# Attention, MoE and routed MoE in one kernel: batch 0's gate logits as VectorE sums over rows read back, and expert 0's w1 loaded whole

## The chip, the cores and the metric

The kernel runs on one core of a Trainium2 chip. The metric is the device time of one execution in microseconds. "Before" is the median of three runs; one further execution was recorded by the hardware profiler, and every row below is from it. Engines are named as in the profile: PE is TensorE's matmul stream, DVE is VectorE, ACT is ScalarE, POOL is GpSimd, and SP is SyncE, which here only issues DMAs.

## What is computed

Attention with a decay over 4 batches of 576 tokens and 8 heads gives x with 2304 rows of 512. Then comes a dense MLP, and then an MLP of 8 experts, 288 tokens each. The expert of a token comes from a greedy walk over all 2304 x 8 gate logits in falling order, so that an exact order of the logits matters.

```python
h = np.maximum(x @ w_in, 0.0)            # _moe_ref: 512 -> 2048
x = (h * h @ w_out).astype(np.float32)   # 2048 -> 512, "x2" below

logits = x @ w_gate                      # _moe2_ref: 512 -> 8
order = np.argsort(-logits.flatten())
for idx in order:                        # first come, first served, 288 tokens each
    tok, e = (int(idx) // E, int(idx) % E)
    if assigned[tok] >= 0 or counts[e] >= cap:
        continue
    assigned[tok] = e
    counts[e] += 1
for e in range(E):
    mask = assigned == e
    out[mask] = np.maximum(x[mask] @ w1[e], 0.0) @ w2[e]
```

## The kernel before

**Stages.** Attention runs by batch and head; its result goes to a DRAM buffer `xd` and is read back as `xa`. The dense MLP works in chunks of 256 tokens: two chunks of batch 0 first, then two of batch 1, two of batch 2 and one of batch 3 (`moe1_chunk`); the last two chunks (`moe1_last`) run together. The batch-0 chunks run while attention of the later heads is still at work, up to about 290 us. The float32 operands are split into a high and a low part (`hh`, `hl` of the hidden values, `xh`, `xl` of the inputs), and each product is three matmuls (L693 to L695 up, L717 to L719 down). Each hidden tile goes PE, then ACT (relu, L698), then a square (L699), then a rounding to `hh`, then a subtraction to `hl` (L710), which VectorE or GpSimd does; the down matmul L719 waits for `hl`.

**Where x2 and the logits come from.** When a chunk is done, its two tiles of 128 tokens are taken from PSUM and stored to `x2d` in DRAM, from which the experts gather their rows later. The logits are made in one of three ways:
- `x2_tail` (batches 0 and 3): 4 transposes on PE (L823), a copy, 8 small matmuls against w_gate (L831; one instruction each of 4 in the listing of the program, 8 in the trace), a copy into `L`.
- `x2_sums` (batches in `DL`, here 1 and 2): 8 instructions on VectorE for a tile (L798), each a multiply with one column of w_gate laid out over all partitions (`wgb`) and a sum over the 512 elements; each is followed by a read of the accumulator.
- in `moe1_last`: from the hidden values through `G2`, the product of w_out and w_gate. `gate_weights` makes `G2` on VectorE beforehand: 16 additions (L850) and 128 of the same sums (L853), which is what VectorE mostly does from about 300 us on. `G2` is finished by L858 and first used by a matmul at about 569 us.

**Who sets the order.** Each engine's order is fixed when the program is built. A list planner places every operation by priority (`s.base`, smaller first) and by modelled durations. `after=` and `hold` are only known to this planner; the hardware waits only for data and buffers. `hi` and `lo` operations have several candidate engines, of which the planner takes one.

**The experts.** The routing of expert m finds its number; SP then reads that number into a register (a value load, L1192) and issues loads of w1 and w2 from that expert's slice (L1204, four tiles each, 512 KB a tile). Before, w1 of the first expert is loaded in halves of 256 KB: the first halves of two tiles when its number is known, the first halves of the other two behind the last x2 store (`WX = 2`, `after=self.x2_done`), all second halves behind the gather. The gather (L1185) is an indirect DMA that GpSimd issues, three of 96 rows of `x2d`. Then PE transposes the rows (L1252) and multiplies (L1272).

Of the kernel before, what the change touches and what calls it, by code (L numbers as in the profile page):

```python
# [8 lines left out]
F = mybir.dt.float32  # L9
R = mybir.dt.float32r  # L10
BF = mybir.dt.bfloat16
# [8 lines left out]
B, H, S, D = 4, 8, 576, 64  # L20
NT, DM, DFF, E, FE = 2304, 512, 2048, 8, 1024
# [11 lines left out]
RS = [("z", z) for z in (31, 30, 29)]  # L33
WS = [("z", 28)]
TM = 1
WX = 2
P0 = None
HV = [0]
NSM = 4

DL = (1, 2)
ABASE = (0, 0.5, 0.6, 2)
HM = 50.0
LM = 40.0
# [278 lines left out]
def dve1(n):  # L323
    return 70 + 1.04 * n
# [46 lines left out]
class K:  # L371
# [355 lines left out]
    def moe1_chunk(self, b, c):  # L727
# [14 lines left out]
        for t in range(2):  # L742
            (self.x2_sums if b in DL else self.x2_tail)(b, c, t, acc[t])

# [45 lines left out]

    def x2_sums(self, b, c, t, acc):
        s = self.s
        xr = s.buf(self.xp, [128, DM], F, "x2g", 0, also=[("xo", 0), ("xo", 1)])
        xr.after = self.gp.bar
        xr, tt = self.x2_rows(b, c, t, acc, xr)
        for x in range(E):
            jk = s.buf(self.gp, [128, DM], BF, "gjs", 1)
            s.op({"dve": dve1(DM) + 285}, lambda e, x=x, jk=jk: e.tensor_tensor_reduce(  # L798
                out=jk.t, in0=xr.t, in1=self.wgb[:, x, :], scale=1.0, scalar=0.0, op0=OP.mult, op1=OP.add,
                accum_out=self.L[:, tt, x:x + 1]), r=[xr, self.wgb], w=[jk, (self.L, tt)])  # L800

    def x2_rows(self, b, c, t, acc, xr=None):
        s, mp = self.s, self.mp
        xr = xr or s.buf(mp, [128, 512], F, "x2r", 0, also=[("wraw", 0), ("wraw", 1)])
        s.op({"act": act(512, True), "dve": dve1(512)}, lambda e: self.rnd(e, xr.t, acc.t), r=[acc], w=[xr])
        tt = (b * 4 + c * 2 if b < B else 16) + t
        if b < B:
            tok = b * S + 64 + c * 256 + t * 128
            self.dma(lambda: self.x2d[tok:tok + 128, :], lambda: xr.t, 128 * 2048, r=[xr], w=[(self.x2d, tt)])
        else:  # L810
            for j in range(2):
                tok = (2 * t + j) * S
                self.dma(lambda tok=tok: self.x2d[tok:tok + 64, :], lambda j=j: xr[64 * j:64 * j + 64], 64 * 2048, r=[xr], w=[(self.x2d, (tt, j))])
        return xr, tt
# [361 lines left out]
    def expert(self, m, idx, widx):  # L1176
        s, nc, ep = self.s, self.nc, self.ep
# [5 lines left out]
        def gather_x():  # L1183
            for g in range(3):
                s.op({"pool": 1040.0}, lambda e, g=g: e.indirect_dma_start(  # L1185
                    out=xg[:, g, :], out_offset=None, in_=self.x2d.t, in_offset=IO(ap=idx[:, g:g + 1], axis=0)),
                    r=[idx, self.x2d], w=[(xg, g)], nbytes=96 * 2048)
# [39 lines left out]
        if m:  # L1227
            for i in range(4):
                wload(0, i)(0, 2)
            s.base = XB + m  # L1230
            gather_x()
            s.base = 30 + m
            for i in range(4):
                wload(1, i)(0, 2)
        else:
            loads = [wload(0, i) for i in range(4)]
            for i in range(4):
                loads[i](0, 1 if 0 in HV else 2, after=self.x2_done if WX <= i else None)
            s.base = X0
            gather_x()  # L1240
            s.base = 30 + m
            if 0 in HV:
                for i in range(4):
                    loads[i](1, 2, hold=True)
            for i in range(4):
                wload(1, i)(0, 2, hold=True)
        s.base = (XB + m if m else X0)
        xh, xl = [], []
        for k in range(4):
            pt = s.buf(self.ps, [128, 512], F, "xt", 0, also=XT + (XA if m == 0 else []))  # L1250
            for g in range(3):
                s.op({"pe": 107.0}, lambda e, k=k, g=g, pt=pt: e.transpose(pt[:, 96 * g:96 * g + 96], xg[:, g, k * 128:k * 128 + 128], self.ident[:96, :96]),  # L1252
                     r=[(xg, g), self.ident], w=[pt])
# [39 lines left out]
        for d in range(4):  # L1293
            acc = s.buf(self.ps, [128, 512], F, "y", 0, also=YA)
# [141 lines left out]
```

## Time and profile before

| | us |
|---|---|
| median of 3 runs | 995.26 |
| the three runs | 993.12, 995.26, 998.85 |
| the profiled execution | 997.44 |
| its span, first to last instruction | 995.7 |

| engine | busy, share of the span |
|---|---|
| PE | 929.3 us, 93% |
| DVE | 637.0 us, 64% |
| ACT | 392.1 us, 39% |
| POOL | 344.9 us, 35% |

The mean granted TensorE clock is 0.972 of full speed. A time in a row is measured from the start of the span. In a line of the timeline the first number is the start, the second the length (of a whole run of like instructions, where xN stands), and the bracket at the end is the idle time of that engine just before, with what ended it.

### The profile page before, as it was taken

What the parts mean: (1) busy time and instruction counts of PE and PEld (TensorE: products, weight loads), DVE (VectorE), ACT (ScalarE), POOL (GpSimd) and SP (SyncE); (2) the same over time, 40 slices, a digit from 0 to 9 for tenths busy, and PEclk for the clock granted to TensorE, in tenths of its full rate; (3) what the DMA queues carried; (4) which work ended last, traced back from release to release, by engine and by line L of the source; (5) the groups of instructions that cost most, each with busy time, mean ns of one, the idle gap of its engine ahead of it and who ended that gap; (6) DMA issues with size and microseconds to landing.
All of it is one profiled execution on the core that took longest, in us unless ns stands there. A gap on an engine that the chain in (4) does not pass through costs nothing. (4 is left out here: it accounts for less than half of the span.)

```text
span 995.7 us, 17474 instructions
## 1 busy us (share of the span) xinstructions
PE 929.3 (93%) x6135; PEld 749.8 (75%) x6135; DVE 637.0 (64%) x2037; ACT 392.1 (39%) x1068; POOL 344.9 (35%) x459
## 2 busy tenths in 40 slices
PE   6897899899999999999999999994999979999996
PEld 3554455677779898989989899774777867778995
DVE  6999888984438999992627322576767786422231
ACT  4665567655634444444343366200101021224320
POOL 2555555653333425341313100001113050557921
PEclk9999899999999999999999999996999998999998
DMA  6668677642230101010100000007735450334410
GB/s 215 206 222 266 197 238 248 194 136 85 75 129 24 44 1 43 1 44 1 43 15 9 22 1 2 11 33 214 241 134 201 176 175 22 111 110 151 133 48 24
DMA packets 48615, 105.66 MB, mean 106 GB/s; under 512 B 10280, under 2 KB 18632, under 8 KB 48400
## 3 DMA queue, kind: packets, MB, share of 16 engines
q1 hardware_dynamic: 45456, 95.11, 29.0%
q0 software_dynamic: 3072, 9.44, 3.2%
q8 instruction: 48, 0.79, 0.3%
q14 instruction: 39, 0.32, 0.1%
HBM read 90.20 MB, written 14.33 MB: 105 GB/s over the span
## 5 line engine op out<-in xcount | busy, mean ns | idle before, releaser
L693 PE MATMUL u<-xh,z 128*128 128x256 f32 x512 | 147.6, 288 | 2.4 <-ACT r L698 1.9
L694 PE MATMUL u<-xh,z 128*128 128x256 f32 x512 | 144.8, 283 | 0.0
L695 PE MATMUL u<-xl,z 128*128 128x256 f32 x512 | 144.7, 283 | 0.0
L698 ACT ACTIVATE r<-u 128x256 f32<-128x256 f32 x144 | 54.6, 380 | 162.7 <-PE u L695 138.0
L710 POOL TENSOR_TENSOR hl<-r,hh 128x256 fp32r<-128x256 f32 x79 | 74.7, 947 | 117.4 <-ACT hh L385 100.7
L853 DVE CUSTOM_DVE_ANT_0 gjk<-wof,wgb 128x512 bf16<-128x512 f32 x128 | 108.1, 845 | 11.0 <-DMA wgb<-wgT 8.0
L693 PEld LDWEIGHTS u<-xh,z 128*128 128x128 f32 x512 | 97.2, 190 | 15.3 <-issue 3.1
L694 PEld LDWEIGHTS u<-xh,z 128*128 128x128 f32 x512 | 97.4, 190 | 8.0
L695 PEld LDWEIGHTS u<-xl,z 128*128 128x128 f32 x512 | 97.3, 190 | 0.0
L1301 PE MATMUL acc<-ehh,z 128*128 128x288 f32 x320 | 91.8, 420 | 0.0
L719 PE MATMUL acc<-z,hl 128*128 128x512 f32 x224 | 88.6, 396 | 2.9 <-POOL hl L710 2.1
L717 PE MATMUL acc<-z,hh 128*128 128x512 f32 x224 | 90.1, 402 | 0.0
L718 PE MATMUL acc<-z,hh 128*128 128x512 f32 x224 | 89.2, 398 | 0.0
L1272 PE MATMUL u<-exh,z 128*128 128x288 f32 x304 | 87.0, 422 | 0.1
L1224 POOL TENSOR_TENSOR z<-wr,z 128x512 fp32r<-128x512 f32 x48 | 61.3, 1312 | 48.1 <-ACT z L385 48.0
L525 ACT ACTIVATE p<-p,st 128x448 f32<-128x448 f32 (+4 forms) x109 | 59.9, 550 | 37.7 <-DVE st L518 37.4
L513 POOL TENSOR_TENSOR row<-maskb,row 128x128 f32<-128x128 bf16 (+1 forms) x90 | 45.8, 516 | 69.0 <-DVE st L518 48.4
L1301 PEld LDWEIGHTS acc<-ehh,z 128*128 128x128 f32 x320 | 57.5, 194 | 16.3 <-issue 2.0
L1272 PEld LDWEIGHTS u<-exh,z 128*128 128x128 f32 x304 | 55.8, 195 | 14.8 <-DVE exh L389 0.3
L1185 POOL DMA_INDIRECT xg<-x2d,ph_idx x24 | 25.6, 1065 | 99.4 <-DVE ph_P L1127 51.9
L699 ACT ACTIVATE r<-r 128x256 f32<-128x256 f32 x139 | 58.0, 418 | 4.2
L1324 POOL DMA_INDIRECT out_dram<-yo,ph_idx x24 | 24.3, 1011 | 100.8 <-DVE ph_q L1034 32.7
(354 smaller groups left out, 2199.2 us busy)
## 6 DMA issues: line engine op xcount, KB each, us to landing
z<-in_w_dram SPq DMA_DIRECT2D x36, 512.0 KB
wr<-in_w_dram SPq DMA_DIRECT2D x24, 512.0 KB
z<-in_w_in_dram SPq DMA_DIRECT2D x16, 512.0 KB
z<-in_w_out_dram SPq DMA_DIRECT2D x14, 512.0 KB
row<-cumd SPq DMA_DIRECT2D x24, 288.0 KB
xd<-xo SPq DMA_DIRECT2D x16, 288.0 KB
wraw<-rd SPq DMA_DIRECT2D x32, 128.0 KB
xa<-xd SPq DMA_DIRECT2D x8, 512.0 KB
```

The lines of the kernel that those rows point to most:

```text
L525: s.op({"act": act(w, extra=2)}, lambda e, x=x, si=si, i=i, n=n, w=w, p=p[x], st=st[x]: e.activation(p[:n, :w], p[:n, :w], AF.Exp, bias=st ...
L693: e.matmul(u[:, :256], wh[:, k % 2, fs], xh[k][1](), start=(k == 0), stop=False)
L694: e.matmul(u[:, :256], wl[:, k % 2, fs], xh[k][1](), start=False, stop=False)
L695: e.matmul(u[:, :256], wh[:, k % 2, fs], xl[k][1](), start=False, stop=(k == 3))
L710: s.op(lo_alts(256), lambda e: e.tensor_sub(hl(), r.t, hh().bitcast(F)), r=[r, kh], w=[kl])
L717: g = [lambda e: e.matmul(acc.t, hh()[:, ts], wh[:, f % 2], start=(f == 0), stop=False), lambda e: e.matmul(acc.t, hh()[:, ts], wl[:, f % ...
L718: lambda e: e.matmul(acc.t, hh()[:, ts], wl[:, f % 2], start=False, stop=False),
L719: lambda e: e.matmul(acc.t, hl()[:, ts], wh[:, f % 2], start=False, stop=(f == 15))]
L853: s.op({"dve": dve1(DM) + 85}, lambda e, f=f, x=x, wo=wo, jk=jk: e.tensor_tensor_reduce(out=jk.t, in0=wo.t, in1=wb[:, x, :], scale=1.0, sc ...
L1224: s.op(lo_alts(512, LOE(m, which, i, 0, c)), lambda e, cs=cs: e.tensor_sub(lo[:, cs], raw[:, cs], hi[:, cs].bitcast(F)), r=[(raw, key), (h ...
L1272: s.op({"pe": 1.69 * CAP}, lambda e, k=k: e.matmul(u[:, :CAP], whi[0][k][:, fs], xh[k].t, start=(k == 0), stop=(k == 3)), r=[(whi[0][k], c ...
L1301: e.matmul(acc[:, :CAP], wh[:, ds], hh.t, start=(f == 0), stop=(f == 7))
```

## The change

Three constants and two functions change. `DL` becomes (0, 1, 2), so batch 0's two chunks (four tiles) take `x2_sums` in place of `x2_tail`. For batch 0 the tile is stored to `x2d` as before, from the same kind of buffer (`wraw`), and then read back from `x2d` into a buffer "x2k" in the space of the attention outputs `xo`; the eight sums of each tile work on that copy and write their products to a buffer of their own ("gjk0"). The read-back and the sums stand at priority 10. Second, `WX` and the split into halves are gone for expert 0: its four w1 tiles are issued whole, one after the other.

```diff
-WX = 2
-DL = (1, 2)
+DL = (0, 1, 2)
     def x2_sums(self, b, c, t, acc):
-        xr = s.buf(self.xp, [128, DM], F, "x2g", 0, also=[("xo", 0), ("xo", 1)])
+        xr = s.buf(self.xp, [128, DM], F, "x2g" if b else "x2k", 0, also=[("xo", 0), ("xo", 1)])
         xr.after = self.gp.bar
-        xr, tt = self.x2_rows(b, c, t, acc, xr)
+        base = s.base
+        if b:
+            xr, tt = self.x2_rows(b, c, t, acc, xr)
+        else:
+
+            _, tt = self.x2_rows(b, c, t, acc)
+            s.base = 10
+            tok = b * S + 64 + c * 256 + t * 128
+            self.dma(lambda: xr.t, lambda: self.x2d[tok:tok + 128, :], 128 * 2048, r=[(self.x2d, tt)], w=[xr])
         for x in range(E):
-            jk = s.buf(self.gp, [128, DM], BF, "gjs", 1)
+            jk = s.buf(self.gp, [128, DM], BF, "gjs" if b else "gjk0", 1)
...
+        s.base = base
...
             for i in range(4):
-                loads[i](0, 1 if 0 in HV else 2, after=self.x2_done if WX <= i else None)
+                loads[i](0, 2)
             s.base = X0
             gather_x()
             s.base = 30 + m
-            if 0 in HV:
-                for i in range(4):
-                    loads[i](1, 2, hold=True)
```

Line numbers of the changed kernel differ: L798 becomes L805, L850 and L853 become L858 and L861, L1192 becomes L1200, L1204 becomes L1212, and lines from 389 to 719 go down by one.

On PE, in the stretch where batch 0's first chunk ends, the order before is this (u and pt are PSUM tiles; L823 is the transpose of an x2 tile, L557 a transpose of attention, L693 to L695 an up product):

```order
939 L557 MATMUL pt_3660<-ident,p_3601 128x128 x3
940 L557 MATMUL ov_3661<-ident,p_3614 128x128 x3
941 L823 MATMUL u_3671<-ident,wraw_3658 128x128 x4
942 L693 MATMUL u_3567<-xh_3552,z_310 128x256
943 L694 MATMUL u_3567<-xh_3552,z_340 128x256
```

and after the change:

```order
939 L556 MATMUL pt_3660<-ident,p_3601 128x128 x3
940 L556 MATMUL ov_3661<-ident,p_3614 128x128 x3
941 L692 MATMUL u_3567<-xh_3552,z_310 128x256
942 L693 MATMUL u_3567<-xh_3552,z_340 128x256
943 L694 MATMUL u_3567<-xl_3572,z_310 128x256
```

The four transposes are gone, and so are those of the three other tiles of batch 0 and the four groups of logit matmuls (L831); the rest of the PE's matmuls to the end of the dense MLP are the same.

On VectorE, where the first sums stand, the order after the change is this ("ISA ... 128x512" is a sum, the "ISA ... 128x1" behind it the read of its accumulator; L805 is a logit of batch 0 from the row tile xo, L861 a sum of `gate_weights`):

```order
725 L805 ISA gjk_3932,L<-xo_3826,wgb_3845 128x512
726 L805 ISA L 128x1
727 L861 ISA gjk_3939,gf_3940<-wof_3796,wgb_3845 128x512
728 L861 ISA gf_3940 128x1
729 L805 ISA gjk_3951,L<-xo_3826,wgb_3845 128x512
730 L805 ISA L 128x1
731 L861 ISA gjk_3964,gf_3940<-wof_3796,wgb_3845 128x512
732 L861 ISA gf_3940 128x1
```

Before, only the sums of `gate_weights` stood in a row here. Further on, where the chunk is that ran at 470 us, the order before is this (L710 makes the `hl` that a down product waits for, L680 an `xl`):

```order
1074 L710 TENSOR_TENSOR hl_5822<-r_5808,hh_5817 128x256
1075 L710 TENSOR_TENSOR hl_5845<-r_5831,hh_5840 128x256
1076 L699 TENSOR_TENSOR r_5862<-r_5862 128x256
1077 L680 TENSOR_TENSOR xl_5872<-xa_4275,xh_5869 128x256
1078 L710 TENSOR_TENSOR hl_5882<-r_5862,hh_5877 128x256
```

and the same hidden tile after:

```order
1109 L861 ISA gjk_5852,gf_3940<-wof_5708,wgb_3845 128x512
1110 L861 ISA gf_3940 128x1
1111 L698 TENSOR_TENSOR r_5859<-r_5859 128x256
1112 L861 ISA gjk_5869,gf_3940<-wof_5708,wgb_3845 128x512
1113 L861 ISA gf_3940 128x1
1114 L709 TENSOR_TENSOR hl_5883<-r_5859,hh_5876 128x256
```

The sums of `gate_weights`, which before ended at the L858 above these rows, now reach beyond them. Counted over the whole listing, before has 152 sums, 14 additions and 6 other operations from the first sum to L858; after has 183 sums, 14 additions and 9 other operations from the first sum to the `hl` of row 1114. The 9 others after are 3 subtractions for `hl`, 4 for `xl` and 2 squares; the 6 before are 4 `hl`, one `xl` and one square. Up to the hidden tile of these rows VectorE makes 13 `hl` before and 4 after: nine go to GpSimd (79 before, 88 after over the whole kernel).

On SP, near `wgb` (the copy of w_gate over all partitions that every sum reads) the order before is

```order
218 L392 DMA wgT<-wraw_3804 8x512
219 L392 DMA xd<-xo_3653 128x576
220 L392 DMA wgb_3845<-wgT 128x4096
221 L392 DMA xa_4275<-xd 128x4x256
```

and after

```order
218 L391 DMA wgT<-wraw_3774 8x512
219 L391 DMA xo_3826<-x2d 128x512
220 L391 DMA wgb_3845<-wgT 128x4096
221 L391 DMA xd<-xo_3653 128x576
222 L391 DMA xo_3945<-x2d 128x512
223 L391 DMA xa_4254<-xd 128x4x256
```

`wgb` is now ahead of the store of xo, and the read-back of the first tile is ahead of `wgb`. At the end of the dense MLP, the four loads of expert 0's w1 (128x1024 now) stand right behind its value load and ahead of the last five x2 stores; the next value load follows those stores, and then the loads of the next expert's w1.

## Rows read from the trace of the kernel before

**Rows 1.** Windows: length, busy PE, PEld, DVE, ACT, POOL, PE clock, DMA share, GB/s
```profile
450.00:475.00 25.00, 25.00 (x159) 22.61 (x158) 6.11 (x15) 10.38 (x26) 2.34 (x4) 1.00 0.06 13
570.00:676.00 106.00, 106.00 (x775) 92.48 (x774) 46.26 (x191) 38.05 (x96) 0.74 (x1) 1.00 0.04 14
676.00:700.00 24.00, 11.31 (x68) 9.31 (x67) 16.51 (x82) 0.73 (x2) 6.79 (x6) 0.58 0.86 262
```

**Rows 2.** Timeline of VectorE: first sum, a long sum, end of gate_weights, an hl
```profile
301.18 0.69 DVE L853 CUSTOM_DVE_ANT_0 gjk<-wof,wgb 128x512 bf16<-128x512 f32 x1 [8.01 <-DMA wgb<-wgT]
...
427.22 1.11 DVE L853 CUSTOM_DVE_ANT_0 gjk<-wof,wgb 128x512 bf16<-128x512 f32 x1
...
442.19 0.47 DVE L858 TENSOR_TENSOR g<-gf,g 128x128 fp32r<-128x128 f32 x1
...
470.74 0.45 DVE L710 TENSOR_TENSOR hl<-r,hh 128x256 fp32r<-128x256 f32 x1
```

**Rows 3.** Timeline of PE: two down products that use an hl of VectorE
```profile
428.73 0.50 PE L719 MATMUL acc<-z,hl 128*128 128x512 f32 x1 [0.53 <-DVE hl L710]
...
471.90 0.39 PE L719 MATMUL acc<-z,hl 128*128 128x512 f32 x1
```

**Rows 4.** Timelines of GpSimd and PE: the first gather, PE's first use
```profile
681.50 1.13 POOL L1185 DMA_INDIRECT xg<-x2d,ph_idx  x1 [51.94 <-DVE ph_P L1127]
...
691.18 0.42 PE L1252 MATMUL pt<-ident,xg 96*128 96x96 f32 x1 [6.30 <-DMA xg<-x2d,ph_idx]
```

**Rows 5.** Timeline of PE, the tails of batch 0's two chunks and what follows them
```profile
279.48 0.60 PE L823 MATMUL u<-ident,wraw 128*128 128x128 f32 x4
279.83 0.37 PE L693 MATMUL u<-xh,z 128*128 128x256 f32 x1
...
281.68 0.65 PE L823 MATMUL u<-ident,wraw 128*128 128x128 f32 x4
282.86 0.30 PE L557 MATMUL pt<-ident,p 64*64 64x64 f32 x2 [0.52 <-DVE pa L389]
...
286.39 0.96 PE L831 MATMUL u<-wg,wraw 128*128 128x8 f32 x8
287.21 0.36 PE L693 MATMUL u<-xh,z 128*128 128x256 f32 x1
...
335.47 0.60 PE L823 MATMUL u<-ident,wraw 128*128 128x128 f32 x4
...
336.74 0.48 PE L717 MATMUL acc<-z,hh 128*128 128x512 f32 x1
...
338.20 1.84 PE L831 MATMUL u<-wg,wraw 128*128 128x8 f32 x16
339.90 0.37 PE L693 MATMUL u<-xh,z 128*128 128x256 f32 x1
```

**Rows 6.** Groups of VectorE by line, from 301.18 to 442.19: count, busy us, mean ns
```profile
L853 DVE CUSTOM_DVE_ANT_0 gjk<-wof,wgb 128x512 bf16<-128x512 f32 x128 | 108.1, 845 | 11.0 <-DMA wgb<-wgT 8.0
L798 DVE CUSTOM_DVE_ANT_0 gjs<-xo,wgb 128x512 bf16<-128x512 f32 x24 | 18.9, 786 | 0.0
L850 DVE TENSOR_TENSOR wof<-z,z 128x512 f32<-128x512 f32 x14 | 12.2, 874 | 0.0
...
L699 DVE TENSOR_TENSOR r<-r 128x256 f32<-128x256 f32 x1 | 0.9, 950 | 0.0
```

**Rows 7.** Timeline of SP: the store of xo, then the load of wgb
```profile
293.20 0.35 SPq L392 DMA_DIRECT2D xd<-xo  x1
293.72 0.34 SPq L392 DMA_DIRECT2D wgb<-wgT  x1
```

**Rows 8.** Timeline of GpSimd beside the long sum of rows 2
```profile
426.73 1.05 POOL L680 TENSOR_TENSOR xl<-xa,xh 128x256 fp32r<-128x256 f32 x1
```

**Rows 9.** Timeline of SP at the end of the dense MLP
```profile
678.96 18.30 SPq L1204 DMA_DIRECT2D z<-in_w_dram  x17
```

**Rows 10.** Chain that ended last: a gather with fewer loads beside it
```profile
929.43 3.15 DMA xg<-x2d,ph_idx
```

## The prediction, made before the changed kernel ran

> **What bounds the kernel now.** I read the shares of busy time first: PE is at work 93% of the span, VectorE 64%. Shares are averages, so next the windows. From the end of attention to the end of the dense MLP PE is full [rows 1]: 25.00 of 25 us, and 106.00 of 106 us at the end of the stage. So an instruction taken off PE before 676 us moves everything behind it forward, unless another engine has been just in time. That is the case to look at: in that part VectorE works through `gate_weights` and the sums of batches 1 and 2, 301.18 to 442.19 us [rows 2], and once PE is seen waiting for it: the down product at 428.73 us stood 0.53 us for an `hl` that VectorE made late [rows 3]. From 450 us VectorE has only 6.11 us of work in 25 [rows 1]. So VectorE's list, where it is full, is the second bound, close behind PE. The third place is the gap between dense MLP and the first expert: PE stands 6.30 us, until 691.18 us, for the gathered rows [rows 4].
>
> **What comes off PE.** Batch 0 has four tiles. Each loses four transposes and eight small matmuls, and I price them by the distance from the group's start to the next group's start [rows 5]. First chunk: 279.48 to 279.83, 0.35 us; 281.68 to 282.34 (where the idle time before 282.86 begins), 0.66 us; 286.39 to 287.21, 0.82 us, and the second such group 0.82 us more (it reads alike). Second chunk: both transposes 335.47 to 336.74, 1.27 us, of which 0.26 us was a wait; the matmuls of both tiles 338.20 to 339.90, 1.70 us. Sum of work 0.35 + 0.66 + 0.82 + 0.82 + 1.01 + 1.70 = 5.4 us, and with the two waits beside them (0.52 and 0.26) 6.1 us. Nothing covers this work now, PE is full around it; I call it 5.8 us that PE can be ahead. The copies behind these groups, on ScalarE and VectorE, also go; neither is late there, so they count nothing.
>
> **What VectorE gets.** 32 sums, each with its read of the accumulator, and the row tiles for them come back from DRAM (256 KB each, on the DMA queue that in this stage is nearly empty). What does one sum cost there? Before, the stretch of 141.01 us [rows 2] holds 152 sums, 14 additions of 12.2 us together [rows 6] and six others: four `hl` at 0.45 us [rows 2], a square at 0.95 us [rows 6] and an `xl`, which I price like the square, 3.7 us. That leaves 125.1 us, or **0.823 us a sum** with its read and all gaps. The bounds are the mean lengths in the rows: 0.786 for the sums of batches 1 and 2, 0.845 for those of `gate_weights` [rows 6]. I take 0.823, for the mixture after is of the same two kinds beside the same amount of GpSimd work per sum.
>
> Now the order: up to the `hl` of the hidden tile that before was made at 470.74 us, after has 183 sums, 14 additions and 9 others. The others are three `hl`, four `xl` and two squares, at the same prices 7.0 us. The start is the arrival of `wgb`, 301.18 before [rows 2]. Its load was issued at 293.72, right behind a store issued at 293.20 [rows 7], and that store now comes after it: 0.52 us for sure, and whatever the store itself had waited for; I take 1.0 in all, so 300.2 us, and half a microsecond more or less here is as much of the lead. Then the `hl` is finished at 300.2 + 183 x 0.823 + 12.2 + 7.0 + 0.45 = **470.5 us**. PE used it at 471.90 before [rows 3]. So VectorE, which had 0.71 us in hand there (470.74 + 0.45 = 471.19), now allows PE to be ahead by 1.4 us at most, where taking the tails away would have given 5.8. Before this row the list allows more (some 3 to 5 us where an `hl` of VectorE is used at 428 us or earlier), after it about 3 us, and behind the last sums VectorE has little to do again [rows 1]; but PE is full from there to 676 us, so what it has lost by then it doesn't win back. The end of `gate_weights` moves some 40 us back, which costs nothing: the chunks of batches 2 and 3 lie between it and the last two chunks, which are the first to use `G2`.
>
> The bounds of this term follow from the bounds of a sum. At 0.786 us the `hl` is ready at 463.5 us, and PE keeps its whole 5.4 to 6.1 us. At 0.845 us it is ready at 474.3 us: PE is 2.4 us later there than before.
>
> What makes a sum long is seen in two rows: the first of the stage lasts 0.69 us [rows 2], one that runs while GpSimd subtracts (426.73 to 427.78) lasts 1.11 us [rows 2, 8]. The change moves nine subtractions for `hl` from VectorE to GpSimd. The Trainium skill says in "GPSIMD Engine Reference", section "1. Specifications", that GpSimd's interface to SBUF is shared with VectorE and that instructions with two SBUF inputs contend for it. That speaks against this change, and the two rows agree with it (0.69 against 1.11 us); by it the second rival below is likelier than a constant price of a sum makes it.
>
> **The w1 loads.** At 678.96 us begins a run of 17 weight loads whose issue takes 18.30 us [rows 9]. Six of these are half tiles of expert 0's w1, 1.5 MB. After, they go out before the last x2 stores, while the dense MLP still runs and the DMA engines are 4% busy [rows 1]. PE did not wait for w1 but for the gathered rows. The gather was issued at 681.50 and its first rows were usable at 691.18, 9.7 us [rows 4]; from the end of issue (682.63) 8.5 us. Far from such loads the same transfer took 3.15 us [rows 10]. So the loads beside it cost up to 5.4 us. But the next expert's four w1 tiles (2 MB) and then expert 0's w2 (2 MB) still go out in this place, with the same engines; only two half tiles (0.5 MB of the 1.5) were ahead of the gather. I give this 0.7 us, from 0 (the other loads take the room) to 2 us (0.5 MB less at the 262 GB/s of this stretch [rows 1]). SP's list: the four loads are ahead of the last five x2 stores, and none of their buffers is in use by then, so the stores aren't held up; were they, the gather would come later by the wait.
>
> The Trainium skill's "DMA: Bandwidth & Descriptors", section "Queues, rings and completion order", says that a DMA engine goes round its queues packet by packet. By that rule a gather takes turns with the weight queue however much stands in it, and the six half tiles would give 0 in place of 0.7 us; 8.5 us against 3.15 us [rows 4, 10] shows that it does lose by the company, but not that it depends on the depth.
>
> **The sum.** 1.4 + 0.7 = 2.1 us off the profiled execution: 997.44 to 995.3 us. The profiled execution is 2.2 us over the median of the three runs, so on their scale the change gives 995.26 - 2.1 = **993.2 us**.
>
> **The rivals.**
> *The whole gain passes.* If a sum takes about 0.80 us or less (at 0.80 the `hl` is ready at 466.0 us, 5.9 ahead of 471.90), PE keeps 5.8 us: 995.26 - 5.8 - 0.7 = 988.8 us. For it: the sums of batches 1 and 2 average 0.786 [rows 6]; and the additional sums run on beyond 450 us, where GpSimd was nearly idle before (2.34 us in 25 [rows 1]). Against it: just that idle time is filled with the nine subtractions that VectorE gives away.
> *VectorE becomes the bound, slower than before.* The place is the same `hl`; it decides from 0.831 us a sum (319.85 + 183 x 0.831 = 471.9). If the 31 additional sums cost 0.97 us, between a long one (1.11) and the mean, then 125.1 + 31 x 0.97 = 155.2 us, `hl` at 475.0, 3.1 us late, and 995.26 + 3.1 - 0.7 = 997.7 us. If all of them last 1.11, `hl` is at 479.4, 7.5 us late, 1002 us. For it: the subtractions that go to GpSimd. Against it: before, too, many sums had such company (the means lie above 0.69), and the 0.823 holds it.
> *The gap gives more.* If the gathered rows come 2 us earlier and PE, which is granted 0.58 of its clock there in the mean [rows 1], gets it back earlier with them, a further 1.5 us may be had, 3.5 from the gap: 995.26 - 1.4 - 3.5 = 990.4 us. Against it: the other 4 MB stay.
> *The second part does nothing*, since other loads take the room: 995.26 - 1.4 = 993.9 us, inside my forecast.
>
> **How the numbers follow.** Forecast, VectorE takes back most of it (990.5 to 995.3): 0.53. The whole gain: 0.20. VectorE the bound: 0.20, most of it under 999, since only an additional sum that is always disturbed gives 1002. The larger gap: 0.07. About 0.5%, 5 us, is what a measurement of this kernel can tell from no change. Faster by more (below 990.3): nearly all of the whole gain, half of the larger gap, and a rest where both add, 0.25. Slower by more (above 1000.2): a third of the second rival, 0.07. Within: 0.68. The range goes from 988.3 (the whole gain and a little more) to 998.0 (the second rival at 0.97 us a sum), and leaves out the far ends of both.
>
> **What would show it.** Right: L823 and L831 gone around 280 to 340 us, PE ahead there by 5 us or more, and that lead shrinking to 1 to 2 us by 472 us, with PE's idle time put down to `hl` on VectorE (or on GpSimd, behind it); a mean distance of sums near 0.82 us; the first transposes of the expert about 9 us after the gather. Wrong: PE without waits between 340 and 480 us (the whole gain), or a lead that is negative at 472 us. In the gap: gathered rows in under 7 us after their issue would make my 0.7 too small. The weakest number is the price of a sum: 1% of it is 1.5 us at the end.

## The result and the profile after

The changed kernel took 987.05 us (median of 6 runs, 986.03 to 990.91), the kernel before 995.67 us beside it (6 runs). The ratio is 0.991, 95% interval 0.9887 to 0.9932; a second comparison gave 0.9884 (0.9847 to 0.9921). So the change made the kernel 9 to 11 us faster, where 2.1 us had been forecast and the range ended 7 us below before. The first profiled execution of the changed kernel took 990.91 us, with a span of 989.1 us.

TensorE is as full as before in the dense MLP, and VectorE is now full to 475 us. Windows of after, columns as in [rows 1]:

```profile
300.00:325.00 25.00, 25.00 (x161) 22.64 (x160) 22.73 (x60) 10.98 (x28) 8.73 (x10) 1.00 0.09 32
...
425.00:450.00 25.00, 25.00 (x163) 22.78 (x162) 25.00 (x65) 11.72 (x29) 9.78 (x10) 1.00 0.06 21
450.00:475.00 25.00, 24.70 (x158) 21.61 (x157) 24.20 (x55) 10.15 (x26) 13.42 (x13) 1.00 0.16 43
475.00:500.00 25.00, 24.88 (x154) 22.39 (x155) 15.65 (x39) 10.46 (x26) 5.63 (x7) 1.00 0.00 1
...
676.00:700.00 24.00, 15.58 (x92) 12.47 (x92) 15.18 (x73) 1.14 (x3) 6.72 (x6) 0.57 0.96 314
```

Against [rows 1], VectorE's busy time between 450 and 475 us rose from 6.11 to 24.20 of 25 us, and GpSimd's from 2.34 to 13.42. So the additional sums and the moved `hl` went where the prediction put them. The two places of [rows 2] read so after (timeline of VectorE, and of PE in the row between, the down product that uses the `hl`):

```profile
302.21 0.69 DVE L805 CUSTOM_DVE_ANT_0 gjk<-xo,wgb 128x512 bf16<-128x512 f32 x1 [7.88 <-DMA wgb<-wgT]
...
465.05 0.95 DVE L709 TENSOR_TENSOR hl<-r,hh 128x256 fp32r<-128x256 f32 x1
...
466.05 0.50 PE L718 MATMUL acc<-z,hl 128*128 128x512 f32 x1
...
479.45 0.81 DVE L866 TENSOR_TENSOR g<-gf,g 128x128 fp32r<-128x128 f32 x1
```

The `hl` that was made at 470.74 before comes at 465.05 now, finished at 466.00: not 0.7 us earlier, as forecast with 470.5, but 5.2 us earlier than the 471.19 of before, and that although the first sum starts 1 us later. In this execution all of attention was some 3 us later than in the profile of before; in a second profile of the changed kernel it was 0.4 us earlier. I therefore take every lead of TensorE as a difference between two points of before, 260 us (ahead of the first matmul that is gone) and 490 us: how much earlier the same matmul starts than in before at the second point, less the same at the first. By that measure TensorE gained 7.9 us between the two points in the first profile of after, and 6.9 us in the second. At 472 us, where I had forecast a lead of 1 to 2 us, it was 8.9 and 7.5 us.

At the end of the dense MLP after has (timelines of GpSimd and PE, as [rows 4])

```profile
678.38 1.13 POOL L1193 DMA_INDIRECT xg<-x2d,ph_idx  x1 [52.12 <-DVE ph_fr L1009]
...
685.89 0.42 PE L1257 MATMUL pt<-ident,xg 96*128 96x96 f32 x1 [4.28 <-DMA xg<-x2d,ph_idx]
```

From the issue of the gather to its first use it is 7.5 us, where [rows 4] have 9.7.

### The profile page after: what moved, and what is told of

The parts are those of the page before. It is cut to its first block, busy times and chain, and to the rows that moved or that the text cites. A ratio compares the mean times of both kernels' runs of the same rounds, so it can differ in the third digit from the quotient of the medians.

```text
span 989.1 us, 17447 instructions
## 1 busy us (share of the span) xinstructions
PE 929.0 (94%) x6087; PEld 747.2 (76%) x6087; DVE 657.5 (66%) x2092; ACT 389.6 (39%) x1058; POOL 353.4 (36%) x470
## 5 line engine op out<-in xcount | busy, mean ns | idle before, releaser
L693 PE MATMUL u<-xh,z 128*128 128x256 f32 x512 | 144.8, 283 | 0.0
L709 POOL TENSOR_TENSOR hl<-r,hh 128x256 fp32r<-128x256 f32 x88 | 84.5, 961 | 118.3 <-ACT hh L384 115.6
L861 DVE CUSTOM_DVE_ANT_0 gjk<-wof,wgb 128x512 bf16<-128x512 f32 x128 | 109.5, 855 | 1.7
L693 PEld LDWEIGHTS u<-xh,z 128*128 128x128 f32 x512 | 97.5, 190 | 8.0
```

Source lines behind the costliest of these rows:

```text
L693: e.matmul(u[:, :256], wl[:, k % 2, fs], xh[k][1](), start=False, stop=False)
L709: s.op(lo_alts(256), lambda e: e.tensor_sub(hl(), r.t, hh().bitcast(F)), r=[r, kh], w=[kl])
L861: s.op({"dve": dve1(DM) + 85}, lambda e, f=f, x=x, wo=wo, jk=jk: e.tensor_tensor_reduce(out=jk.t, in0=wo.t, in1=wb[:, x, :], scale=1.0, sc ...
```

## The experiments

Each table row below is worked out from one profiled execution, by the lead defined above, against the first profile of before; the stretch behind it runs from the end of the last down product to the end of the span. Medians are of the kernel and of before beside it.

| kernel | lead gained, 260 to 490 us | last down product to end, us | median, us | before beside it |
|---|---|---|---|---|
| before, second profile | +0.2 | 317.1 (first: 318.9) | 999.1 | 999.13 |
| after, first and second profile | -7.9, -6.9 | 315.6, 315.9 | 987.05, 988.1 | 995.67, 999.13 |
| first part alone | -6.7 | 318.6 | 990.99 | 996.36 |
| second part alone | -0.4 | 313.4 | 993.64 | 996.36 |
| batch 0's sums short | -6.7 | 316.0 | 986.55 | 996.36 |
| batch 0's sums twice | +15.8 | 319.0 | 1013.55 | 996.36 |
| before, all sums short | -4.0 | 318.4 | 994.58 | 997.28 |
| after, all sums short | -10.5 | 316.5 | 985.69 | 997.28 |
| eight more sums | -1.0 | 318.1 | 996.59 | 997.28 |
| w1 whole but late | -6.9 | 317.0 | 989.03 | 997.28 |
| sums planned longer | -6.8 | 315.2 | 990.72 | 999.13 |
| batch 0's sums later | -5.9 | 319.1 | 992.03 | 999.13 |

A minus is a gain. Of five profiles with the changed kernel's order up to 490 us, the one with batch 0's sums short among them, four give -6.7 to -6.9 and one -7.9, 7.0 in the mean. A difference of less than a microsecond between two single profiles is therefore not told from noise.

**The two parts apart.** First part alone:

```diff
+WX = 2
-                loads[i](0, 2)
+                loads[i](0, 1 if 0 in HV else 2, after=self.x2_done if WX <= i else None)
...
+            if 0 in HV:
+                for i in range(4):
+                    loads[i](1, 2, hold=True)
```

> Only the first part of the change: batch 0's logits as sums, expert 0's w1 in halves as before. Theory A (the matmuls that leave TensorE carry the gain, and VectorE keeps up): 6 to 7.5 us under before, about 988.5 to 989.5 us where before is 995.5; the end of the dense MLP 6 us or more earlier than before's 676.8, less what a drop of the clock takes. Theory B (the loads carry it): within 2 us of before, 993.5 to 996.

It took 990.99 us, ratio 0.9959 (0.9928 to 0.9989). Its lead of 6.7 us is that of the whole change, and behind the dense MLP it takes 318.6 us, like before. Theory A holds for the trace; the end of the dense MLP came 5.7 us earlier than before's, a little less than expected. The median is 1.5 us over the expected band.

The second part alone is the kernel before with `loads[i](0, 2)` and without the halves:

> Only the second part: expert 0's four w1 tiles whole and early, batch 0's logits on TensorE as before. Theory A: 1 to 2.5 us under before, 993 to 994.5 us where before is 995.5, the gap between the last down product and the first product of the expert 1 to 2 us shorter, nothing ahead of it. Theory B: 6 us or more under before, 989 or less.

993.64 us, ratio 0.9972 (0.9949 to 0.9995). As theory A has it, there is next to nothing ahead of the gap (-0.4 us), and the stretch from the last down product to the first expert product is 17.8 us against 19.3. Theory B is out: the greater part of the change's gain is the first part's.

**Does VectorE's list hold TensorE?** In the first pair only the work of batch 0's sums differs, the order of every engine is that of the changed kernel:

```diff
+            n = DM if b else 64
-                out=jk.t, in0=xr.t, in1=self.wgb[:, x, :], scale=1.0, scalar=0.0, op0=OP.mult, op1=OP.add,
+                out=jk[:, :n], in0=xr[:, :n], in1=self.wgb[:, x, :n], scale=1.0, scalar=0.0, op0=OP.mult, op1=OP.add,
```

> The changed kernel in its own order, but batch 0's 32 sums run over 64 of the 512 elements (so these logits are other numbers). About 32 x 0.6 = 19 us leave VectorE's list by 466 us. Theory A (VectorE kept up): 0.5 to 1.5 us under the changed kernel, by the waits of TensorE between 338 and 476 us (1.5 us in all), 985.5 to 987 us. Theory C (VectorE still took back part of the gain): 3 us or more under the changed kernel, 984 or less.

986.55 us, lead -6.7 us: nothing gained, though VectorE was busy 18.7 us less between 300 and 500 us. Where the time went is told by VectorE's own waits from 300 to 480 us (us in total, times, longest), in this kernel

```profile
DVE r L698 <- ACT r L697: 10.3, 2, 10.1
DVE xl L679 <- ACT xh L384: 10.2, 1, 10.2
```

and in after

```profile
DVE xl L679 <- ACT xh L384: 1.4, 1, 1.4
DVE r L698 <- ACT r L697: 0.2, 1, 0.2
```

The 19 us became two waits of 10 us: VectorE came early to operations that wait for ScalarE, which here follows TensorE's pace, and could not go past them. So batch 0's 32 sums cost TensorE nothing in the changed kernel.

With the same sums emitted twice (`for _ in range(1 if b else 2)` around the instruction):

> The changed kernel in its own order, each of batch 0's 32 sums made twice. 32 x 0.79 = 25 us more on VectorE by the hl that TensorE needs at 466 us. Theory A with no room left at that place (TensorE stood 0.09 us there): 20 to 25 us over the changed kernel, 1007 to 1012 us, TensorE standing for hl and for ScalarE behind it between 330 and 480 us. Theory D (VectorE has much room, its list was never near the bound): under 995 us.

1013.55 us, a little over the expected band. The lead turns from about -7 to +15.8 us: 23 us for 32 further sums, 0.72 us each, all of it on TensorE. Its waits from 300 to 490 us (PE alone):

```profile
PE u L694 <- DVE xl L679: 19.3, 2, 10.0
PE acc L718 <- POOL hl L709: 0.4, 1, 0.4
```

The waits are for `xl`, the low part of the next chunk's input, at two places; for the `hl` on which my prediction was built TensorE stands 0.09 us here, as in the first profile of after (in the second 0.60). A quarter of this dose, the sums of two columns of eight (`x % 4 == 0`) made twice:

> The changed kernel in its own order, 8 of batch 0's 32 sums made twice: 8 x 0.79 = 6.3 us more on VectorE. All 32 made twice put 25 us more there and 22 us on TensorE, so some 3 us of room were left. Theory A with that room: TensorE 3 to 4 us later at 460 us than in the changed kernel, 990 to 991.5 us. Rival (waits cost more than the last one shown): 6 us, 993.

996.59 us, and the lead shrinks from about -7 to -1.0 us: 6 us for 6 us of sums. On the lead the rival was right, there are no 3 us of room; the median is 3.6 us above its 993. Waits of PE from 300 to 500 us:

```profile
PE u L694 <- DVE xl L679: 4.1, 2, 2.8
PE acc L718 <- POOL hl L709: 0.9, 3, 0.4
PE acc L718 <- DVE hl L709: 0.5, 1, 0.5
```

So the list is filled but for the 1.6 us that VectorE itself waits in after (above): the 32 sums of the change were nearly free, and from there on each further sum costs about its full length.

**What VectorE costs TensorE before and after.** All sums over 64 elements, in the order of before and of after; this is the edit of `gate_weights`, and `x2_sums` has the same one:

```diff
-                    out=jk.t, in0=wo.t, in1=wb[:, x, :], scale=1.0, scalar=0.0, op0=OP.mult, op1=OP.add,
+                    out=jk[:, :64], in0=wo[:, :64], in1=wb[:, x, :64], scale=1.0, scalar=0.0, op0=OP.mult, op1=OP.add,
```

> The kernel before in its own order, all sums of gate_weights and of batches 1 and 2 over 64 of the 512 elements (so logits are other numbers): VectorE is empty for most of 301 to 442 us. Theory A (before, the full list of VectorE held TensorE up at 329, 333, 383, 426 and 429 us, 2.7 us in all, and the change took these waits away too): TensorE 2.5 to 3 us earlier at 500 us, 992.5 to 994 us where before is 996. Rival (these waits were GpSimd's or the planner's order): less than 1 us, 995 or more.

994.58 us, ratio 0.9974 (0.9944 to 1.0004). The interval of the time takes in no change at all; the lead is 4.0 us, more than expected. TensorE's waits for `hl` in before, apart from the one of [rows 3],

```profile
329.57 0.50 PE L719 MATMUL acc<-z,hl 128*128 128x512 f32 x1 [0.21 <-POOL hl L710]
...
333.00 0.50 PE L719 MATMUL acc<-z,hl 128*128 128x512 f32 x1 [0.69 <-POOL hl L710]
...
382.66 0.50 PE L719 MATMUL acc<-z,hl 128*128 128x512 f32 x1 [0.70 <-POOL hl L710]
...
426.15 0.50 PE L719 MATMUL acc<-z,hl 128*128 128x512 f32 x1 [0.54 <-POOL hl L710]
```

are gone in it, and what is left of waits between 300 and 500 us is 0.3 us for a step of ScalarE. Four of the five waits are put down to GpSimd, whose instructions had the sums for company, not to VectorE's list. The two `xl` and the `hl` ahead of the first of these waits (GpSimd, in before)

```profile
326.18 2.20 POOL L680 TENSOR_TENSOR xl<-xa,xh 128x256 fp32r<-128x256 f32 x2
328.34 1.18 POOL L710 TENSOR_TENSOR hl<-r,hh 128x256 fp32r<-128x256 f32 x1
```

are much shorter with short sums:

```profile
327.44 1.51 POOL L680 TENSOR_TENSOR xl<-xa,xh 128x256 fp32r<-128x256 f32 x2
328.95 0.74 POOL L710 TENSOR_TENSOR hl<-r,hh 128x256 fp32r<-128x256 f32 x1
```

> The changed kernel in its own order, all sums over 64 elements. GpSimd's subtractions for hl then have no company on VectorE. Theory E (the 1.2 us that TensorE loses between 466 and 482 us come from hl made on GpSimd beside the sums): this loss and the waits at 420 and 423 us go, 1.5 to 2.5 us under the changed kernel, 984.5 to 985.5. Rival (the loss is in the planner's order or on ScalarE): the lead falls by 1.2 us there as before, and the time is within 1 us of the changed kernel.

985.69 us; the lead is 10.5 us, 3.5 us more than the 7.0 of the changed kernel's order. Between 466 and 482 us, where after loses 1.3 us against before, this kernel loses 0.4. That agrees with theory E, as far as one profile tells.

**Where the second part's gain lies.** `loads[i](0, 2, after=self.x2_done)` leaves w1 whole and lets the planner put the loads behind the last x2 store:

> The changed kernel with expert 0's w1 loads whole, but held by the planner until the last x2 store, so that they go out in the gap as before. GpSimd's order of the weight splits in the expert stage is then like the changed kernel's, not like before's (3 splits, not 8, ahead of the fourth expert's stores). Theory F (the second part's gain is 2 us in the gap and some 3 us by the other order of these splits): the gap is as long as before (14.3 us from the last down product to the first transpose), the expert stage as short as in the changed kernel, 988 to 990 us. Rival (all of it is in the gap): 991 us, like the first part alone.

989.03 us, ratio 0.9897 (0.9866 to 0.9929). The time is theory F's, but its reasons don't fit: the rows come 12.6 us after the last down product and 7.9 us after the gather's issue, much as in the changed kernel, though these loads go out in the gap as before's do; but the first product waits 5 us longer (22.6 us, 17.6 in after), and the expert stage behind it takes 294.5 us, against 297.9 in after and 299.6 in before. The loads change not only the gap but the planner's order of the expert stage, and the two can't be had apart by this edit.

What that order does is seen around 810 us. With before's loads GpSimd has a long run of splits (timelines of POOL, DVE and PE in the first part alone)

```profile
806.24 9.11 POOL L1233 TENSOR_TENSOR z<-wr,z 128x512 fp32r<-128x512 f32 x6 [3.06 <-ACT z L385]
...
805.96 0.56 DVE L1055 TENSOR_TENSOR ph_G<-ph_bb,rc_i 128x768 bf16<-128x768 bf16 x1
...
812.62 1.61 DVE L1055 TENSOR_TENSOR ph_G<-ph_bb,rc_i 128x768 bf16<-128x768 bf16 x1
...
814.28 0.80 PE L1066 MATMUL ov<-ph_G,ph_OH 128*128 128x128 bf16 x6 [2.58 <-DVE ph_G L1055]
```

and in after two of them:

```profile
807.57 2.81 POOL L1232 TENSOR_TENSOR z<-wr,z 128x512 fp32r<-128x512 f32 x2 [3.92 <-ACT z L384]
...
811.19 0.55 DVE L1054 TENSOR_TENSOR ph_G<-ph_bb,rc_i 128x768 bf16<-128x768 bf16 x1
...
811.79 0.51 PE L1065 MATMUL ov<-ph_G,ph_OH 128*128 128x128 bf16 x6 [0.43 <-DVE ph_G L1054]
```

The routing's instruction on VectorE takes 0.55 us alone and 1.61 us beside the splits, and TensorE waits for it. In all nine profiles with whole and early loads TensorE gains 6.4 to 7.5 us between 800 and 830 us of before, 0.2 to 1.1 us in those with before's loads; most of that is lost again between 830 and 935 us. I take it that the splits of later experts stand there instead; no run tests it. What stays of the expert stage (first product to end) is 299.3 to 299.9 us in four profiles with before's loads, 295.5 to 301.3 us (the middle one 298.3) with whole and early ones.

**Repeats.**

> The kernel before once more, for a second profile: TensorE stands again for hl near 329, 333, 383, 426 and 429 us, 2 to 3 us in all; from the last down product to the end 318 to 319.5 us; 993 to 999 us.

999.1 us, with the waits for `hl` where they were expected, 2.7 us in all. But it took 317.1 us behind the last down product, less than expected, for the gap was 1.6 us shorter than in the first profile of the same kernel:

```profile
683.71 1.13 POOL L1185 DMA_INDIRECT xg<-x2d,ph_idx  x1 [51.95 <-DVE ph_P L1127]
...
691.80 0.42 PE L1252 MATMUL pt<-ident,xg 96*128 96x96 f32 x1 [4.72 <-DMA xg<-x2d,ph_idx]
```

8.1 us from issue to use, where [rows 4] have 9.7. So the gap varies from run to run as much as the second part may change it.

> The changed kernel once more, for a second profile. From before's 266 us to 490 us TensorE gains 7 to 8 us on the first profile of before (7.8 in the first profile of the changed kernel, 6.7 to 6.9 in three others with the same order up to there); the time from the last down product to the end is 315 to 318 us, where kernels with before's loads had 318.4 to 318.9; 986 to 989 us.

988.1 us and 315.9 us as expected, and a lead of -6.9 us, just short of the 7 to 8.

**Two attempts to win the waits back.** One line each, `dve1(DM) + 285` in place of `+ 85` for the sums of `gate_weights`, and `s.base = 12.5` in place of 10 for batch 0's:

> The changed kernel, but the planner reckons a sum of gate_weights 0.2 us longer (as long as it reckons those of the logits), so that it puts fewer of them between two steps that TensorE waits for. All sums short gave 2.7 to 3.5 us on TensorE between 300 and 490 us. Theory G (the waits come from too many sums between two such steps): 1.5 to 3 us of that come back, 984 to 986 us. Rival (the same work only moves to another place): within 1 us of the changed kernel.

> The changed kernel with batch 0's sums at priority 12.5, behind gate_weights, where before's VectorE was idle from 450 us. Theory G: up to 3 us less waiting of TensorE between 300 and 440 us, 984 to 986 us. Rival (gate_weights and the other sums still fill every gap between two steps): within 1 us of the changed kernel.

990.72 us (ratio 0.9927, 0.9896 to 0.9958) and 992.03 us (0.992, 0.9894 to 0.9947); leads -6.8 and -5.9 us. Neither is better than the changed kernel, so theory G is out. The medians lie 2.6 and 3.9 us above the 988.1 us of the changed kernel in the same comparison, further off than the 1 us of the rivals; why they are slower stays open.

## Why the prediction was wrong, point by point

- **What comes off PE: right in kind, a little small.** Both kernels with all sums short have TensorE next to free of VectorE and differ by 10.5 - 4.0 = 6.5 us. I had 5.8 us, from 5.4 to 6.1; the 0.4 to 0.7 us between is within the scatter of single profiles.
- **What VectorE gets: this step failed.** I forecast that VectorE would allow 1.4 us of the 5.8. In fact the toll that VectorE and its company take from TensorE was 4.0 us before and 10.5 - 7.0 = 3.5 us after: it did not rise. So TensorE got about 7.0 us, the whole gain.
- **The mis-sized term is the price of a sum.** By the distances between the starts of neighbouring instructions, before the 152 sums took 126.8 us, 0.834 us each (my 0.823 was near); after, 183 sums took 145.5 us, **0.795 us each**. So 31 more sums cost VectorE 18.7 us, 0.60 us each. Two groups of lines show where that comes from (VectorE, before and then after):

```profile
303.18 0.69 DVE L853 CUSTOM_DVE_ANT_0 gjk<-wof,wgb 128x512 bf16<-128x512 f32 x1
303.80 0.08 DVE L853 DVE_READ_ACCUMULATOR2_ANT gf<- 128x1 f32 x1
303.91 0.69 DVE L853 CUSTOM_DVE_ANT_0 gjk<-wof,wgb 128x512 bf16<-128x512 f32 x1
...
302.83 0.69 DVE L861 CUSTOM_DVE_ANT_0 gjk<-wof,wgb 128x512 bf16<-128x512 f32 x1
303.45 0.08 DVE L861 DVE_READ_ACCUMULATOR2_ANT gf<- 128x1 f32 x1
303.45 0.68 DVE L805 CUSTOM_DVE_ANT_0 gjk<-xo,wgb 128x512 bf16<-128x512 f32 x1
```

  A sum that follows one of its own group starts 0.11 us after the start of the accumulator's read; a sum of another group, which writes another product buffer, starts together with the read. This is so for every such pair in both traces. In the stretch counted here there are 86 pairs of the first kind before (9.8 us) and only 44 after (5.0 us), since sums of batch 0 and of `gate_weights` now stand by turns. From the start of a sum to its read it is 0.765 us before and 0.758 after. At before's 0.834 the 183 sums would have taken 7.2 us longer: 6.8 us of that are the gaps behind the reads, 1.4 us the shorter sums, and 1.0 us went the other way into waits of VectorE. The order that I had on record shows the two groups by turns; I counted kinds of sums and not neighbours. Whether the shared product buffer or the accumulator makes the gap, no run separates.
- **GpSimd's company stayed in proportion.** The groups (VectorE, 302 to 465.5 us of after, as [rows 6]):

```profile
L861 DVE CUSTOM_DVE_ANT_0 gjk<-wof,wgb 128x512 bf16<-128x512 f32 x119 | 100.7, 846 | 1.5
L805 DVE CUSTOM_DVE_ANT_0 gjk<-xo,wgb 128x512 bf16<-128x512 f32 x32 | 25.8, 805 | 7.9 <-DMA wgb<-wgT 7.9
L805 DVE CUSTOM_DVE_ANT_0 gjs<-xo,wgb 128x512 bf16<-128x512 f32 x32 | 24.8, 776 | 0.0
```

  A sum lasted 0.835 us in the mean before and 0.827 after; over 0.9 us lasted 47 of 152 before and 51 of 183 after. GpSimd's busy time beside them rose from 57.6 to 70.0 us, by about as large a share as the number of sums. So this part of the working held. Batch 0's sums were disturbed too, 0.805 us in the mean against 0.69 alone.
- **The same working with the measured terms.** Start 302.21 in place of 300.2 (+2.0; without the 3.0 us by which attention was late here, it would be -1.0), sums 145.5 in place of 150.6 (-5.1), the nine others 5.2 in place of 7.0 (-1.8), the `hl` itself 0.95 in place of 0.45 (+0.5), additions 12.2 as forecast. That is 466.0 where I had 470.5, and 471.9 - 466.0 = 5.9 us ahead of before at that place; TensorE's product stands at 466.05, 5.85 us ahead. In three places my sums are 0.2 us too low: with 319.85 us as the rest, the `hl` is ready at 463.7, 474.5 and 466.2 us for sums of 0.786, 0.845 and 0.80 us.
- **The place was the wrong one too.** Added sums make TensorE wait for `xl` near 330 and 380 us (eight more sums), and not for the `hl` at 470 us. And the 471.90 us of [rows 3] that I measured against was no free pace: TensorE had lost 4 us on the way there, of which I had read a single wait of 0.53 us. The four waits for an `hl` of GpSimd, 2.1 us, stood in the same trace.
- **Rivals.** The whole gain passing, the one with 0.20, was the case; its condition (a sum at 0.80 us or less) was met with 0.795. VectorE as the bound was not the case, but its mechanism exists, at the `xl` and not at the `hl`: eight more sums cost 6 us, 32 more 23 us. The larger gap was not the case either, see below.
- **The trend that the sharing rule gave.** By "GPSIMD Engine Reference", "1. Specifications", of the Trainium skill, I held the second rival likelier. The rule agrees with the rows (1.11 us beside GpSimd's subtraction, 0.69 us alone), but it says nothing on how often that happens. Here the share of long sums did not rise, though nine subtractions went to GpSimd, and the second rival was not the likelier one.
- **The w1 loads: size as forecast, not resolved.** The gap from the last down product to the first product is 17.7, 18.4, 19.1 and 19.3 us in the four profiles with before's loads and 17.6 to 18.0 us, once 19.2, in the nine with whole early ones: 0.7 us in the mean, the 0.7 that I had, but two runs of one kernel differ by 1.6. From issue to first use the gather takes 8.1 to 9.7 us in those four and 7.4 to 9.0 in the nine, and 7.9 where whole loads went out in the gap. A depth of the queue that matters is thus neither shown nor excluded. The 3.15 us of [rows 10] were not free of loads either: from 926 to 934 us the DMA engines moved 143 GB/s.
- **Left out: the expert stage.** I took it as unchanged. Its order on GpSimd does change with the loads, and kernels with whole early loads are about 1 us shorter there (298.3 against 299.5 us in the middle), with a spread of several us. Together with the gap the second part is worth 2 to 3 us: 2.7 by its own median.
- **The sum.** 7.0 us up to 490 us and 2 to 3 us behind the dense MLP make 9 to 10, against 8.6 and 11.0 us measured.

What stays open is how the second part's 2 to 3 us divide between the gap and the order of the splits, and what makes the gap behind a read.

## What to carry to other kernels

Price an addition to a full queue by the neighbours that it will have in the new order, not by the mean of the instructions already there: the mean of 0.83 us held a gap behind the read that the added sums filled, and 31 more sums cost 0.60 us each. Before measuring an added delay against the time at which an engine was served, ask whether that time was itself late: add up all waits on the way, whichever engine they are put down to. And an edit to one load can move a planner's choices 150 us further on, so look there at the order of every engine.

## What the runs showed of the hardware

- A VectorE instruction on 128x768 bf16 with two inputs took 0.55 us alone and 1.61 us while GpSimd subtracted float32 tiles; a sum on 128x512 float32 took 0.69 us alone and 1.10 to 1.23 us. The short bf16 instruction loses a factor of three, the float32 one less than two.
- A sum on VectorE started 0.11 us after the start of the accumulator's read behind the sum before it where both wrote the same product buffer, and together with that read where the buffers differed: 118 and 45 pairs in the whole trace of before, 69 and 127 in that of after, without an exception.
- GpSimd lost by the sums as they by it: its 128x256 float32 subtraction took 0.74 us with short sums and 1.18 us beside long ones.
- VectorE could be filled to between 22.7 and 25.0 of 25 us from 300 to 475 us with TensorE losing only some 3.5 us by it, and eight sums more (6 us) then cost TensorE 6 us.
- Between two profiled executions of the same kernel before, the first use of the gathered rows came 9.7 and 8.1 us after the issue.
